# Transposed scores and reordered norms in the first batch of a cross-covariance attention and feed-forward kernel

## The chip, the cores and the metric

The kernel runs on one core of one Trainium2 chip. A core has TensorE for matmuls (PE in the profile, with its weight loads as PEld), VectorE (DVE), ScalarE (ACT), GpSimd (POOL, which here mostly issues DMAs) and SyncE (SP, likewise). They run independently and wait for one another on semaphores. Sixteen DMA engines move data between HBM and the on-chip memory SBUF; matmuls write into PSUM.

The metric is device time in microseconds (us), lower is better. The span of a profile, from the first to the last instruction, is a little shorter than the measured time.

## The reference

Two parts in a row. Cross-covariance attention makes, for each of 4 batches, a 256 x 256 matrix from q and k, and multiplies v with it. A feed-forward part with squared relu follows.

```python
B, N, C = (4, 6080, 256)
qn = q / (np.linalg.norm(q, axis=1, keepdims=True) + 1e-06)
kn = k / (np.linalg.norm(k, axis=1, keepdims=True) + 1e-06)
s = kn.transpose(0, 2, 1) @ qn / tau          # 256 x 256 per batch
s = s - s.max(-1, keepdims=True)
a = np.exp(s)
a /= a.sum(-1, keepdims=True) + 1e-09
x = (v @ a)                                   # then (24320, 256)

h = x @ w_in                                  # (256, 2048)
r = np.maximum(h, 0.0)
g = moe_s * (r * r) + moe_b
out = g @ w_out                               # (2048, 256)
```

The norms are taken over the 6080 rows, so each of the 256 columns of q and of k has one norm for a batch. They, and the scores, need all rows of q and k: nothing of a batch's feed-forward part can start before its last rows are there.

## The kernel before

The kernel folds the attention matrix into the first weights: it computes `wa = softmax(...) @ w_in`, so that `h = v @ wa` (line 641 of its source), squares the relu, and computes `g @ w_out` (lines 687, 713, 809; for most groups of 512 rows in a form with seven instead of eight half-size products). The attention of batch 0 comes first, as a prologue. That of batches 1 to 3 is spread, a step at a time, over the feed-forward work of the batch before.

q and k come in chunks of 512 rows (128 partitions x 4 rows x 256), cast to fp16 by the DMA; the first two chunks come as fp32 and are cast on DVE and ACT. In batch 0 the last rows make two chunks of 2 rows a partition. The scores are collected in one PSUM tile, with k as the stationary operand:

```python
def mm(self, c, j):
    ...
    for ch in range(CH):
        po(nc.tensor.matmul(
            self.s_ps[:, ch, :],
            kc[:np_, j, ts(ch, P)],
            qc[:np_, j, :],
            ...
```

`po` keeps an instruction in the order of the program. For the norms, k is squared on ACT and q on DVE; DVE folds the four rows of a partition into one, and PE sums over the partitions with a column of ones (one column of output a matmul):

```python
def squares(a, js):
    def f():
        ...
        if a == 0:
            po(nc.vector.tensor_mul(sq[:np_, 0, js, :], qc[:np_, js, :], qc[:np_, js, :]))
        else:
            po(nc.scalar.activation(out=sq[:np_, 1, js, :], in_=kc[:np_, js, :], func=AF.Square))
...
def add_norms(self, arrays=(0, 1), last=False):
    ...
        for i, (t, np_, j, ch) in enumerate(todo):
            po(nc.tensor.matmul(self.n_ps[a][:, ch : ch + 1], t[:np_, a, j, ts(ch, P)],
                                ones16[:np_, 0:1], ...))
```

In batch 0 every chunk's folded rows are summed on PE; in later batches an accumulating DMA adds them to the first chunk's rows (`into_first`).

The norms are roots by `Ln` and `Exp(0.5 x)` on ACT; DVE adds EPS and takes the reciprocal. The scores are scaled by k's inverse norms and must be turned over so that q's columns lie on the partitions: on PE in batch 0 (`turn`), in later batches by splitting into two fp16 parts and transposing those with DMAs (`split`, `join`). `exps` then applies q's inverse norms as the activation's scale:

```python
def scale():                                   # batch 0
    for ch in range(CH):
        po(nc.vector.tensor_scalar_mul(out=st["s"][:, ch], in0=self.s_ps[:, ch],
                                       scalar1=st["r"][:, 1, ch : ch + 1]))
def turn():
    ...
    for ch in range(CH):
        for j in range(CH):
            po(nc.tensor.transpose(st["t"][j][:, ts(ch, P)], st["s"][:, ch, ts(j, P)], ident32))
def exps(j):
    po(nc.scalar.activation(out=st["e"][:, j, :], in_=st["t"][j], func=AF.Exp,
                            scale=st["r"][:, 0, j : j + 1]))
def sums():                                    # row sums r_ps, reciprocal rs
    ...
def fold_mm(f0, n, m, wa_ps):                  # wa = e.T @ w_in, then scaled by rs
    ...
```

The prologue's program order, with matmuls on idle data (`keep_busy`, called fillers below) between the chunks:

```python
NFILL = 3
FILL = {-9: 2, -8: 2, -7: 2, -6: 4, -5: 4, -4: 4, -3: 2}
...
for c in range(NCH0 - 2):
    ops = g0.norm_ops(c)
    if c >= NCH0 - 3:
        g0.add_norms()
    for j in range(g0.chunks[c][2]):
        g0.mm(c, j)
    fill = FILL.get(c - NCH0, 0)
    if fill:
        keep_busy(fill, ...)
    for f in ops:
        f()
...                                            # k's squares and norms of the last two chunks
fin[0]()
fin[1]()
keep_busy(NFILL, ...)
for c in (NCH0 - 2, NCH0 - 1):
    ops[c - NCH0 + 2][1]()                     # q's squares
    for j in range(g0.chunks[c][2]):
        g0.mm(c, j)
for f in fin[2:5]:                             # q's norms, scale, reciprocal
    f()
fin[5]()                                       # turn
transpose_v(0)
keep_busy(2, w_in16[:, 0, :P], w_in16[:, 0, :NW])
for f in fin[6:12]:                            # exps, sums, first parts of wa
    f()
```

Of the kernel before, what the change touches and what calls it, by code (L numbers as in the profile page):

```python
# [16 lines left out]
def kernel(  # L17
# [32 lines left out]
    SHIFT = 3  # L50
    assert CH == 2 and FT == 16
# [14 lines left out]
    sq_pool = pool("sq_pool", 2)  # L66
    f3_pool = pool("f3_pool", 13)
# [41 lines left out]
    class Gram:  # L109
# [32 lines left out]
        def mm(self, c, j):  # L142
            qc, kc = self.tiles[c]
            _, np_, jc = self.chunks[c]
            for ch in range(CH):
                po(nc.tensor.matmul(  # L146
                    self.s_ps[:, ch, :],
                    kc[:np_, j, ts(ch, P)],
                    qc[:np_, j, :],
                    start=(c == 0 and j == 0 and ch == 0),  # L150
                    stop=(c == len(self.chunks) - 1 and j == jc - 1 and ch == CH - 1),
                    skip_group_check=True,
                ))

        def norm_ops(self, c):
# [4 lines left out]

            def squares(a, js):
                def f():
                    if "sq" not in st:
                        st["sq"] = sq_pool.tile([P, 2, JC, C], FP16, tag="sq", name="sq")
                    if a == 0:
                        po(nc.vector.tensor_mul(  # L166
                            st["sq"][:np_, 0, js, :], qc[:np_, js, :], qc[:np_, js, :]))
                    else:
                        po(nc.scalar.activation(  # L169
                            out=st["sq"][:np_, 1, js, :], in_=kc[:np_, js, :], func=AF.Square))  # L170
                return f

            def fold(half, arrays, last):
                def f():
# [10 lines left out]
                    if last and (self.b == 0 or c == 0 or c == len(self.chunks) - 1):  # L185
# [4 lines left out]
            def into_first():  # L190

                dst, src = self.rows[0][0][0][:np_], st["f", 1][:np_]
                po(nc.gpsimd.dma_start(out=dst, in_=src, accum_op=ALU.add))  # L193

            def unfolded():
                for rows in self.rows:
                    rows.append((st["sq"], np_, jc))
# [5 lines left out]
            if jc == 2:  # L203
# [4 lines left out]
            return ops + [into_first] if self.b > 0 and 0 < c < len(self.chunks) - 1 else ops  # L208

        def add_norms(self, arrays=(0, 1), last=False):  # L210

            if self.b > 0:

                self.n_all = x_tile[0][:, 1, : 2 * CH].rearrange("p (a c) -> p a c", a=2)
                self.n_ps = [self.n_all[:, 0], self.n_all[:, 1]]
            for a in arrays:
                first = self.n_ps[a] is None
                if first:
                    self.n_ps[a] = ps_o.tile([P, 2, C], FP32, tag="o_ps", name="n_ps")[:, 0, :CH]
                todo = [(t, np_, j, ch) for t, np_, jc in self.rows[a] for j in range(jc)  # L220
                        for ch in range(CH)]
                self.rows[a].clear()
                for i, (t, np_, j, ch) in enumerate(todo):
                    po(nc.tensor.matmul(self.n_ps[a][:, ch : ch + 1], t[:np_, a, j, ts(ch, P)],
                                        ones16[:np_, 0:1], start=(first and i == 0),
                                        stop=(last and i == len(todo) - 1),
                                        skip_group_check=True))

        def finish_ops(self):
# [3 lines left out]
            def root(out, sums):  # L233

                po(nc.scalar.activation(out=out, in_=sums, func=AF.Ln, bias=tiny))
                po(nc.scalar.activation(out=out, in_=out, func=AF.Exp, scale=0.5))

            def norms(a=None):

                if "r" not in st:  # L240
                    st["nrm"] = sm_pool.tile([P, 2, CH], FP32, tag="nrm", name="nrm")
                    st["r"] = sm_pool.tile([P, 2, CH], FP32, tag="rnrm", name="rnrm")
                if a is None:
                    self.add_norms(last=True)
                    root(st["nrm"], self.n_all)
                else:
                    self.add_norms((a,), last=True)
                    root(st["nrm"][:, a], self.n_ps[a])

            def recip(a=None):  # L250
                own = slice(0, 2) if a is None else slice(a, a + 1)
                nrm, r = st["nrm"][:, own], st["r"][:, own]
                po(nc.vector.tensor_scalar_add(out=nrm, in0=nrm, scalar1=EPS))
                po(nc.vector.reciprocal(out=r, in_=nrm))
                if inv_tau != 1.0 and a != 1:
                    po(nc.vector.tensor_scalar_mul(
                        out=st["r"][:, 0], in0=st["r"][:, 0], scalar1=inv_tau))

            def scale():
                st["s"] = sm_pool.tile([P, CH, C], FP32, tag="sm_s", name="sm_s")  # L260
                for ch in range(CH):
                    po(nc.vector.tensor_scalar_mul(
                        out=st["s"][:, ch], in0=self.s_ps[:, ch],
                        scalar1=st["r"][:, 1, ch : ch + 1]))


            def split(part):
                st[part] = sm_pool.tile([P, CH, C], FP16, tag=f"s_{part}", name=f"s_{part}")
                rk = st["r"][:, 1]
                if part == "hi":  # L270
                    po(nc.vector.tensor_mul(
                        st["hi"], self.s_ps, rk[:, :, None].broadcast_to((P, CH, C))))
                else:
                    for ch in range(CH):
                        po(nc.vector.scalar_tensor_tensor(
                            out=st["lo"][:, ch], in0=self.s_ps[:, ch], scalar=rk[:, ch : ch + 1],
                            op0=ALU.mult, in1=st["hi"][:, ch], op1=ALU.subtract))
                st[part + "T"] = sm_pool.tile([P, CH, C], FP16, tag=f"t_{part}", name=f"t_{part}")
                for ch in range(CH):
                    po(nc.sync.dma_start_transpose(  # L280
                        out=st[part + "T"][:, :, ts(ch, P)], in_=st[part][:, ch, :]))

            def join():
                t_sb = sm_pool.tile([P, CH, C], FP32, tag="sm_s", name="t_sb")
                po(nc.vector.tensor_add(t_sb, st["hiT"], st["loT"]))
                st["t"] = [t_sb[:, j, :] for j in range(CH)]

            def turn():

                st["t"] = [h_tile("t_ps")[:, 0, :C], self.bank("t_ps", CH, C)[:, 0, :]]  # L290
                for ch in range(CH):
                    for j in range(CH):
                        po(nc.tensor.transpose(
                            st["t"][j][:, ts(ch, P)], st["s"][:, ch, ts(j, P)], ident32))

            def exps(j):
                if j == 0:
                    st["e"] = sm_pool.tile([P, CH, C], FP16, tag="eT", name="eT")
                po(nc.scalar.activation(
                    out=st["e"][:, j, :], in_=st["t"][j], func=AF.Exp,  # L300
                    scale=st["r"][:, 0, j : j + 1]))
# [53 lines left out]
            if self.b == 0:  # L355
                front = [lambda: norms(1), lambda: recip(1), lambda: norms(0),
                         scale, lambda: recip(0), turn]
            else:
                front = [norms, recip]
                front += [lambda: split("hi"), lambda: split("lo"), join]  # L360
# [46 lines left out]
    ident32 = consts.tile([P, P], FP32)  # L407
    make_identity(nc, ident32)
# [12 lines left out]
    nc.vector.memset(tiny, 1e-30)  # L421
    for c in range(NDIRECT):
        g0.load(c)
        g0.cast(c)
    for c in range(NDIRECT, len(g0.chunks) - 2):
        g0.load(c)

    for parts in ((0,), (1,)):
        for c in range(len(g0.chunks) - 2, len(g0.chunks)):
# [7 lines left out]
    load_w_in(0, NW)  # L437
    load_v(0)
    load_w_in(NW, 2 * NW)
# [20 lines left out]
    NFILL = 3  # L460
    FILL = {-9: 2, -8: 2, -7: 2, -6: 4, -5: 4, -4: 4, -3: 2}

    def keep_busy(n, w, x):

        idle_ps = h_tile("idle_ps")[:, 0, :]
        for _ in range(n):
            po(nc.tensor.matmul(idle_ps, w, x, start=True, stop=True, skip_group_check=True))

    fin = g0.finish_ops()
    for c in range(NCH0 - 2):  # L470
        ops = g0.norm_ops(c)
        if c >= NCH0 - 3:
            g0.add_norms()
        for j in range(g0.chunks[c][2]):
            g0.mm(c, j)
        fill = FILL.get(c - NCH0, 0)
        if fill:
            keep_busy(fill, g0.tiles[c][1][:, 0, :P],
                      g0.tiles[c][0][:, :2, :].rearrange("p j c -> p (j c)"))
# [3 lines left out]
    ops = [g0.norm_ops(c) for c in (NCH0 - 2, NCH0 - 1)]  # L483
    g0.add_norms()
    for k_squares, _, into_rows in ops:
        k_squares()
        into_rows()
    fin[0]()
# [412 lines left out]
```

## Time and profile before

| what | value |
|---|---|
| time, median of 3 runs | 719.0 us (719.0 to 719.15) |
| span of the profile | 717.2 us, 17629 instructions |
| first h matmul (line 641) | 38.60 us |
| scores, PE line 146 | 384 matmuls, 69.6 us |
| ACT squares, line 169 | 49, 50.4 us, 1033 ns each |
| DMA, whole span | 84.25 MB, mean 117 GB/s |
| DMA, first 38.6 us | 221 GB/s |

How to read it: a group's line gives the source line, the engine, what is written from what, the count, the busy time and the mean of one. A timeline's line gives the start, the duration, engine and line, the operation, and in brackets how long the engine was idle before and what ended that. The chain of waits runs back from the last instruction through whatever released each step, and is printed in order of time: start, duration, engine, line. The "granted clock" is what the throttle allowed TensorE, as a share of full speed.

### The profile page before, as it was taken

The numbers are of one execution on the slowest core, as the hardware profiler recorded it, in microseconds if no ns is written. First come the engines' busy times: TensorE is split into PE (matmuls) and PEld (weight loads), VectorE is DVE, ScalarE is ACT, GpSimd is POOL, SyncE is SP. The second block draws the span as 40 slices with busy tenths as digits, with TensorE's granted clock in tenths as the row PEclk, the third lists the DMA queues.
The fourth block names the chain that finished last, engine by engine and source line by source line (L and its number), as shares of the span: only waits on it lengthen the run. The fifth ranks groups of instructions, "written<-read, shape, count | busy, mean of one in ns | idle before, by whom it ended". The sixth has DMA issues, their size and how long they took to land.

```text
span 717.2 us, 17629 instructions
## 1 busy us (share of the span) xinstructions
PE 698.9 (97%) x7479; PEld 504.6 (70%) x7479; DVE 626.1 (87%) x882; ACT 536.5 (75%) x579; POOL 109.8 (15%) x189
## 2 busy tenths in 40 slices
PE   4799999999999999999999999999999999999998
PEld 2556777776677777777677777777668777777777
DVE  4879999999789999999889899999887888888886
ACT  4479877787777777777777778777877777777875
POOL 4532332101201222111110222110000000000000
PEclk9999999999999999999999999999999999999999
DMA  9999998647556879443972877944423333321201
GB/s 236 207 259 172 159 170 137 111 108 129 119 107 114 144 133 145 108 93 83 154 151 57 141 138 124 154 90 86 105 63 75 93 71 74 97 60 46 83 30 74
DMA packets 89790, 84.25 MB, mean 117 GB/s; under 512 B 59664, under 2 KB 64848, under 8 KB 89712
## 3 DMA queue, kind: packets, MB, share of 16 engines
q0 software_dynamic: 26064, 43.40, 37.5%
q1 hardware_dynamic: 63072, 38.43, 21.5%
q8 instruction: 58, 0.95, 0.6%
q10 hardware_dynamic: 576, 1.31, 0.5%
q14 instruction: 20, 0.16, 0.1%
HBM read 78.91 MB, written 24.90 MB: 145 GB/s over the span
## 4 chain that ended last, share of the span: by engine, by line
PE 93%; DMA 4%; DVE 1%; ACT 1%; POOL 1%; issue 0%; POOLq 0%; ACTq 0%
PE h_ps L641 45%; PE o_ps L809 40%; PE s_ps L146 4%; DMA qk<-in_q_dram 3%; PE wa_ps L326 2%; DMA v<-in_v_dram 1%; PE o_ps L713 1%; PE o_ps L687 0%; POOL qk L130 0%; ACT r L651 0%; DVE o_sb L669 0%; DVE S L737 0%; DVE sq L166 0%; DVE S L735 0%; DVE S L739 0%
## 5 line engine op out<-in xcount | busy, mean ns | idle before, releaser
L651 ACT ACTIVATE r<-h_ps 128x1024 f16<-128x1024 f32 (+1 forms) x384 | 388.4, 1014 | 153.4 <-PE h_ps L641 150.9
L641 PE MATMUL h_ps<-vT,wa 128*128 128x512 f16 (+7 forms) x1632 | 452.1, 364 | 0.1
L809 PEld LDWEIGHTS <-S 128*128 128x128 f16 x2944 | 198.0, 98 | 85.0 <-issue 0.9
L809 PEld LDWEIGHTS <-g 128*128 128x128 f16 x2208 | 155.0, 98 | 74.1
L664 DVE TENSOR_TENSOR g<-r 128x2048 f16<-128x2048 f16 (+2 forms) x150 | 174.8, 1165 | 14.6 <-ACT r L651 14.5
L809 PE MATMUL o_ps<-T,S 128*128 128x128 f16 x2208 | 183.3, 219 | 0.1
L641 PEld LDWEIGHTS <-wa 128*128 128x128 f16 x1632 | 135.9, 98 | 20.6 <-ACT wa L319 0.3
L809 PE MATMUL o_ps<-w_out,g 128*128 128x128 f16 x1472 | 134.2, 219 | 0.2 <-DVE u L669 0.2
L669 DVE SCALAR_TENSOR_TENSOR o_sb<-o_ps,s_out,u 128x256 f32<-128x256 f32 x138 | 66.5, 482 | 47.1 <-PE o_ps L809 44.5
L662 ACT ACTIVATE g<-r 128x1024 f16<-128x1024 f16 (+1 forms) x97 | 100.4, 1035 | 0.2
L146 PE MATMUL s_ps<-qk 128*128 128x256 f16 (+1 forms) x384 | 69.6, 281 | 14.0 <-ACT qk L137 8.7
L379 POOL DMA_DIRECT2D v<-in_v_dram x48 | 31.3, 656 | 263.5 <-DMA vT<-v 209.6
L669 DVE SCALAR_TENSOR_TENSOR u<-o_ps,s_out,rowconst 128x256 f32<-128x256 f32 x138 | 66.0, 478 | 0.0
L809 PE MATMUL o_ps<-w_out,S 128*128 128x128 f16 x736 | 63.5, 219 | 0.0
L809 PE MATMUL o_ps<-N,g 128*128 128x128 f16 x736 | 63.4, 219 | 0.0
L193 POOL DMA_DIRECT2D f<-f x30 | 26.3, 877 | 225.6 <-DVE f L182 172.0
L169 ACT ACTIVATE sq<-qk 128x1024 f16<-128x1024 f16 (+3 forms) x49 | 50.4, 1033 | 10.0 <-DMA qk<-in_k_dram 6.7
L737 DVE TENSOR_TENSOR S<-S,g 128x2048 f16<-128x2048 f16 (+1 forms) x47 | 56.4, 1201 | 1.3
L735 DVE TENSOR_TENSOR S<-g 128x2048 f16<-128x2048 f16 (+1 forms) x47 | 56.1, 1193 | 0.0
L741 DVE TENSOR_TENSOR S<-g,S 128x2048 f16<-128x2048 f16 x46 | 56.0, 1217 | 0.0
L739 DVE TENSOR_TENSOR S<-g 128x2048 f16<-128x2048 f16 x46 | 55.9, 1216 | 0.0
L146 PEld LDWEIGHTS <-qk 128*128 128x128 f16 (+1 forms) x384 | 32.8, 101 | 20.1 <-DVE qk L136 8.0
(74 smaller groups left out, 314.9 us busy)
## 6 DMA issues: line engine op xcount, KB each, us to landing
out_dram<-o_sb SPq DMA_DIRECT2D x46, 512.0 KB, 3.0
v<-in_v_dram POOLq DMA_DIRECT2D x47, 256.0 KB, 4.7
qk<-in_k_dram POOLq DMA_DIRECT2D x42, 256.0 KB, 6.1
qk<-in_q_dram POOLq DMA_DIRECT2D x42, 256.0 KB, 7.2
f<-f POOLq DMA_DIRECT2D x30, 128.0 KB, 3.1
vT<-v SPq DMA_TRANSPOSE x182, 3.2
w<-in_moe_w_out_dram POOLq DMA_DIRECT2D x4, 512.0 KB, 11.3
raw<-in_k_dram SPq DMA_DIRECT2D x2, 512.0 KB, 6.4
```

What stands on the lines that cost most here:

```text
L146: po(nc.tensor.matmul(self.s_ps[:, ch, :], kc[:np_, j, ts(ch, P)], qc[:np_, j, :], start=(c == 0 and j == 0 and ch == 0), stop=(c == len(s ...
L169: po(nc.scalar.activation(out=st["sq"][:np_, 1, js, :], in_=kc[:np_, js, :], func=AF.Square))
L641: po(nc.tensor.matmul(dst, wa[:, ci, ts(m, P)], src, start=(ci == 0), stop=(ci == CH - 1), skip_group_check=True))
L651: po(nc.scalar.activation(out=r16[:, :, i % 2, :n], in_=h_tiles.pop((g, i))[:, :, :n], func=AF.Relu))
L662: po(nc.scalar.activation(out=dst, in_=src, func=AF.Square))
L664: po(nc.vector.tensor_mul(dst, src, src))
L669: po(nc.vector.scalar_tensor_tensor(out=dst, in0=src, scalar=s_out, op0=ALU.mult, in1=add, op1=ALU.add))
L735: po(nc.vector.tensor_add(T[1], A21, A22))
L737: po(nc.vector.tensor_sub(T[2], T[1], A11))
L739: po(nc.vector.tensor_sub(T[3], A11, A21))
L741: po(nc.vector.tensor_sub(T[4], A12, T[2]))
L809: po(nc.tensor.matmul(st[name][:, j, :], a()[:, i, ts(j, P)], w[:, i, :], start=first, stop=last, skip_group_check=True))
```

## The change

The change touches the attention part, for the most part batch 0.

- The operands of the score matmul are exchanged, so that the scores come out with q's columns on the partitions, as the exponential wants them. The transposes on PE, and the split, the transposing DMAs and the join of the later batches, are left out.
- k's norms then lie along the free dimension. They are wanted in every partition, so k's sums are taken with a 128 x 128 matrix of ones as the stationary operand and 256 columns of output; q's sums stay as they were.
- The inverse norms come from ACT alone: Ln, Exp(0.5 x), Ln with EPS as bias, Exp(-x). Add and reciprocal on DVE are left out.
- In batch 0 both q and k are squared on ACT, apart from the last three chunks, whose q squares and small k squares are DVE's. DVE folds them and adds the folded rows to those of the first chunk, so that PE sums one tile and not one for each chunk.
- The last three chunks (`NLATE`) have k's rows loaded ahead of q's, and k's norms are finished before q's last rows come. The first v tile is loaded ahead of w_in, whose first 512 columns come in two pieces.
- The fillers are left out, apart from two of 256 columns before the first parts of wa. One identity matrix (fp32) is no longer made.
- In later batches the finishing steps are laid out anew (`FIN`, `fin_len` 56 instead of 54).

The diff, cut to its core; cuts are marked with "...":

```diff
@@ mm
-                    kc[:np_, j, ts(ch, P)],
-                    qc[:np_, j, :],
+                    qc[:np_, j, ts(ch, P)],
+                    kc[:np_, j, :],
@@ norm_ops
+            at_end = self.b == 0 and c >= len(self.chunks) - NLATE
...
-                    if a == 0:
+                    if a == 1 and at_end and jc < JC:
+                        po(nc.vector.tensor_mul(
+                            st["sq"][:np_, 1, js, :], kc[:np_, js, :], kc[:np_, js, :]))
+                    elif a == 0 and (self.b > 0 or at_end):
                         po(nc.vector.tensor_mul(
                             st["sq"][:np_, 0, js, :], qc[:np_, js, :], qc[:np_, js, :]))
                     else:
                         po(nc.scalar.activation(
-                            out=st["sq"][:np_, 1, js, :], in_=kc[:np_, js, :], func=AF.Square))
+                            out=st["sq"][:np_, a, js, :], in_=(qc, kc)[a][:np_, js, :],
+                            func=AF.Square))
...
             def into_first():
-                dst, src = self.rows[0][0][0][:np_], st["f", 1][:np_]
-                po(nc.gpsimd.dma_start(out=dst, in_=src, accum_op=ALU.add))
+                dst, src = self.first[:np_], st["f", 1][:np_]
+                if self.b == 0:
+                    po(nc.vector.tensor_add(dst, dst, src))
+                else:
+                    po(nc.gpsimd.dma_start(out=dst, in_=src, accum_op=ALU.add))
@@ add_norms
+                if a == 1:
+                    po(nc.tensor.matmul(self.n_ps[1], ones16[:np_, :], t[:np_, 1, j],
+                                        start=start, stop=end, skip_group_check=True))
+                    continue
...
@@ finish_ops: root, recip, split, join, turn go
+            def inverse(a):
+                def part(i):
+                    ...
+                    func, kw = [(AF.Ln, dict(bias=tiny)), (AF.Exp, dict(scale=0.5)),
+                                (AF.Ln, dict(bias=eps)), (AF.Exp, dict(scale=-1.0))][i]
+                    po(nc.scalar.activation(out=r, in_=r if i else self.n_ps[a], func=func, **kw))
...
+            def scale(halves=1):
+                ...
+                    po(nc.vector.tensor_mul(st["t"][:, js], self.s_ps[:, js],
+                                            rk[:, None, :].broadcast_to((P, n, C))))
...
@@ loads
-    load_w_in(0, NW)
     load_v(0)
+    load_w_in(0, 2 * P)
+    load_w_in(2 * P, NW)
@@ prologue
-    NFILL = 3
-    FILL = {-9: 2, -8: 2, -7: 2, -6: 4, -5: 4, -4: 4, -3: 2}
...
+    for c in range(NCH0 - NLATE):
         ops = g0.norm_ops(c)
-        if c >= NCH0 - 3:
-            g0.add_norms()
         for j in range(g0.chunks[c][2]):
             g0.mm(c, j)
...
+    for c in late:
+        k_squares, _, into_rows = ops[c]
         k_squares()
-        into_rows()
+        into_rows(1)
+        g0.add_norms(1)
+    for f in last_sums:                        # last fold and add of chunk NCH0 - 4
+        f()
...
+    for f in (norms_k, *inverse_k):
+        f()
+    for c in late:
+        ops[c][1]()                            # q's squares
+        ops[c][2](0)
         for j in range(g0.chunks[c][2]):
             g0.mm(c, j)
+        if c == NCH0 - 1:
+            norms_q()
+        else:
+            g0.add_norms(0)
+    for f in inverse_q:
         f()
+    scale_s()
     transpose_v(0)
-    keep_busy(2, w_in16[:, 0, :P], w_in16[:, 0, :NW])
+    keep_busy(w_in16[:, 0, :P], w_in16[:, 0, : 2 * P])
+    keep_busy(w_in16[:, 0, :P], w_in16[:, 0, : 2 * P])
...
-    FIN = (0, 3, 5, 7, 15, 17, 19, 22)
+    FIN = (0, 0, 3, 5, 7, 16, 16, 17, 18, 19, 20, 24, 26, 29)
```

## The prediction

> **What bounds the kernel now.** First the page: busy time by engine and the slices, to see which engine fills the span and where it does not.
>
> ```profile
> PE 698.9 (97%) x7479; PEld 504.6 (70%) x7479; DVE 626.1 (87%) x882; ACT 536.5 (75%) x579; POOL 109.8 (15%) x189
> ...
> PE   4799999999999999999999999999999999999998
> ```
>
> TensorE (PE) is full from the fourth slice on. A busy PE need not be a PE at its peak, so I asked for the busy time by stretch, cut where the first matmul of the feed-forward part starts (38.60 us in the timeline).
>
> ```profile
> 0.00:38.60 38.60, 23.88 (x206) 16.10 (x206) 24.32 (x50) 18.24 (x24) 20.16 (x41) 1.00 1.06 221
> 38.60:60.00 21.40, 21.35 (x130) 12.29 (x131) 17.91 (x31) 18.92 (x22) 4.47 (x9) 1.00 1.09 226
> 60.00:700.00 640.00, 639.67 (x6961) 463.48 (x6959) 572.30 (x782) 491.19 (x522) 85.18 (x140) 1.00 0.57 109
> 700.00:717.20 17.20, 13.96 (x189) 12.71 (x186) 11.55 (x22) 8.20 (x14) 0.00 (x0) 1.00 0.21 77
> ```
>
> The columns are length, then PE, weight loads, DVE, ACT and POOL with counts, then granted clock, DMA share and GB/s. From 60 to 700 us PE is idle for 0.33 us of 640. The stretches around the later batches' changeovers (150 to 200, 330 to 380, 510 to 560 us) have 50.00 of 50 us. So what the change does for batches 1 to 3, on DVE, ACT or in transposes, has no idle PE to recover. Only the first 38.6 us can move: a prologue, then a full PE stream whose length the change hardly touches.
>
> The chain of waits says what the prologue is:
>
> ```profile
> 4.35 11.56 DMA qk<-in_q_dram
> ...
> 18.76 9.74 DMA qk<-in_q_dram
> 28.50 0.28 issue
> 28.78 7.72 DMA v<-in_v_dram
> 36.50 0.05 issue
> 36.55 0.62 PE vT_ps L390 x8
> 37.17 0.43 PE idle_ps L467 x2
> 37.60 0.08 PE r_ps L309 x4
> 37.68 0.90 PE wa_ps L326 x8
> 38.57 0.02 issue
> 38.60 0.60 PE h_ps L641 x2
> ```
>
> Loads of q and k up to 28.5 us, then v, then a few matmuls. The timeline has a second path beside it, almost as long, from the last rows of q to the exponentials:
>
> ```profile
> 34.00 0.24 DVE L253 TENSOR_SCALAR nrm<-nrm 128x2 f32<-128x2 f32 x1 [1.08 <-ACT nrm L236]
> ...
> 34.35 0.74 DVE L166 TENSOR_TENSOR sq<-qk 128x512 f16<-128x512 f16 x2
> ...
> 35.44 0.26 ACT L235 ACTIVATE nrm<-n_ps,tiny 128x2 f32<-128x2 f32 x1 [1.47 <-PE n_ps L224]
> ...
> 36.43 0.84 ACT L299 ACTIVATE eT<-t_ps,rnrm 128x256 f16<-128x256 f32 x2 [0.50 <-PE t_ps L293]
> ```
>
> DVE runs in order and sits 1.08 us behind ACT's root of k's norms before it may square q's last rows. The exponentials end at 37.27, and v's transposes and the two fillers at 37.60: removing either path alone gains at most 0.3 us.
>
> [...] records of the 128x256 score matmul are 418 ns at 7 to 13 us and 272 ns from 14.3 us, after a run that began at 10.61. No trace here shows PE falling back, since the fillers kept it busy. The granted-clock column reads 1.00 throughout, so this is read from durations. [...] the trace's 128x2048 f16 products take 1218. So folds, squares and the new in-place add cost what the same shapes cost now. [...] The trace's 128x2 Ln takes 0.26 us, and the 128x256 exponential 0.47 from PSUM and 0.50 from SBUF. [...] the trace has one table load, at the start.
>
> **The change part by part.**
>
> *Loads.* Same bytes. In the steady part a 512 KB piece lands every 1.25 us (q's pieces release PE at 26.0 and 28.5, with one of k between). I put k's last large piece at 29.8 (its square starts at 29.82) and q's last piece at 34.0, estimated back from v at 36.5 in two steps of 1.25. Reordered, I estimate k's pieces at 29.8, 30.55 and 31.15, and q's at 32.4, 33.2 and 34.0. v now precedes w_in, so it lands about 35.25 instead of 36.5, and the first quarter of w_in near 36. Its transposes (0.62 us) then end before the exponentials, which takes v off the chain.
>
> *Squares on ACT.* Ten chunks at two 128x1024 squares: three back to back took 2.94 us, so 0.98 each, 1.96 a chunk against 2.5 us between chunks. ACT starts late (10.5 us, after its second cast) with four chunks waiting: twenty squares from 10.5 at 0.98 is 30.1, just behind the last of these q pieces at 28.5. It catches up only at the end. DVE: folds of 0.69 and 0.42 plus a new add of 0.42 is 1.53 a chunk instead of 0.68+0.69+0.42 = 1.79. Both fit under the loads.
>
> *k's norms early.* Last fold 30.0 to 30.7, two k squares (0.40 each) to 31.55, fold and add (0.42 each) to 32.45, nine ones matmuls of 256 columns finishing near 32.8. Then four dependent 128x256 activations; from 0.47 for one of this shape I estimate 1.85 us: k's inverse norms by 34.7.
>
> *q's end.* PE must do eight score matmuls, ten one-column sums, four score matmuls, four sums, again four and four. From 32.8, with 0.107 us a score matmul (eight in 1.03 us with the drain) and 28 ns a sum (forty in 1.14), the last sum is near 35.1 and ready at 35.25. The sum on PE binds rather than the landing at 34.0. Then four 128x2 activations in place of Ln, Exp, add and reciprocal: 0.26+0.20+0.26+0.20 plus gaps, about 1.0, against 0.94 now (35.44 to 36.34 with handovers). Exponentials start 36.0 to 36.3 instead of 36.43, since the inverse norms now bind. DVE scales in two halves of 0.48 from 34.95, so this is done at 35.9. It replaces the two scalings and four fp32 transposes (0.74 us), the path that ended at 36.38.
>
> *To the first h matmul.* Exponentials from SBUF take 0.50 each instead of 0.42 apart, ending 37.0 to 37.3; the present stretch from r_ps at 37.44 to h_ps at 38.60, 1.16 us, stays. First h matmul: 38.2 to 38.5. Gain 0.1 to 0.4 us; I take 0.35 with the earlier first load issue (one identity fewer on POOL).
>
> *After that.* For each later batch, eight one-column sums (0.22 us) become two of 256 columns and four of one (0.33): 0.3 us more PE in all. Gone are DVE's 0.68+0.95+0.69+0.34 us, about 2.7, and four transposing DMAs, against a product of about 0.7 and some 1.4 us more ACT; DVE and ACT have room there. The wait for w_in's last half (40.5 us) is met, since its fold comes at about 41. Sum: 719.0 - 0.35 + 0.3 = 718.95. A shorter DVE queue may take back part of the 0.33 us that PE idles from 60 to 700; I give it half, 0.15: **718.8 us**.
>
> **Rivals.** *PE goes cold.* Without fillers PE works 0.86 us in each 2.5. Every gap is near 1.6 us[...]; but the least that PE was seen to stay warm on is 0.86+0.43 of 2.5. If cold, the sixteen last score matmuls take 0.21 us, the q sums end about 1.5 us later, and the stream starts 1 to 2 us late: 720 to 720.6. [...] *ACT becomes the bound.* If ACT's backlog does not close by 30 us, k's sums and four long activations slip one for one: 719 to 720. For it: only 0.5 us a chunk to spare; against: the count above. *The loads hide it all.* If v and w_in land no sooner, nothing moves: 719.0 to 719.3. *DVE relief pays.* If PE in the steady part has waits that the busy column hides, 717.5 is possible; 0.33 us idle of 640 speaks against.
>
> **Range and chances.** Most of the weight lies on a shift of under half a microsecond either way; perhaps three in ten on a cold or late prologue worth 1 to 2 us. So 717.6 to 720.4. Two per cent is 14.4 us, over a third of the prologue, and nothing found reaches it.
>
> **What would show it.** In the profile after: score matmul records of 272 ns from 16 to 35 us (warm) or 418 (cold); v's transposes before 36.2; ACT's ones-summed Ln near 32.9; exponentials starting 36.0 to 36.3; the first h matmul at 38.2 to 38.5; PE idle under 1 us from 60 to 700. The prediction is wrong if the first h matmul lies after 39, or if the stream from there to the end is not within 0.5 us of the present 678.6 (717.2 - 38.6) with the 0.3 added.

## The result and the profile after

The changed kernel takes 724.2 us (median of 5 runs, 723.88 to 725.31) against 719.03 us: a ratio of 1.0074, 95% interval 1.0062 to 1.0087. It is 0.7% slower, within 2%, and outside the predicted range of 717.6 to 720.4.

The page of the kernel after: busy time by engine, and from the 40 slices those of PE and of the clock that the throttle granted, in tenths.

```profile
PE 700.7 (97%) x7413; PEld 504.4 (70%) x7413; DVE 619.6 (86%) x863; ACT 550.5 (76%) x609; POOL 110.3 (15%) x188
...
PE   4799999999999999999999999999999999999997
PEclk9699999999999999999999999999999999999999
```

PE is 97% busy, as before. Its clock has a dip in the second slice (18 to 36 us). Busy time by stretch of the kernel after, cut at its first h matmul (39.35 us):

```profile
0.00:39.35 39.35, 22.92 (x146) 14.99 (x146) 20.77 (x46) 27.59 (x36) 20.53 (x40) 0.83 1.08 221
39.35:60.00 20.65, 20.59 (x126) 11.72 (x126) 17.23 (x30) 18.22 (x21) 4.47 (x9) 1.00 1.08 223
60.00:700.00 640.00, 637.52 (x6896) 460.74 (x6894) 565.58 (x762) 492.62 (x538) 85.33 (x140) 1.00 0.59 108
```

The prologue is 0.75 us longer (39.35 against 38.60 us). From there to the end the stream takes 723.5 - 39.35 = 684.15 us, where it took 717.2 - 38.60 = 678.6: **5.55 us more**. The busy column shows 2.48 us of PE idle from 60 to 700 us, against 0.33, so it explains less than half of that.

**Where the stream lost it.** I set the start of each relu activation (384 in each kernel, in the same order) against its counterpart before. The delay is 0.75 us at the first, and nearly the same up to 88 us. For batch 1 it grows by 0.53 us between 88 and 142 us and by 1.28 at the finishing steps. For batches 2 and 3 it grows by 0.18 before and by 1.38 at the finishing steps, each time. That is 4.93 us, in a few places, three times over. The other 0.64 us comes after the last matmul: from its start to the end of the span it is 4.11 us, and 3.47 before.

**What happens there.** The timeline of the kernel after at batch 1's finishing steps (start, duration, engine and line, operation; weight loads and work of no bearing are cut):

```profile
146.13 0.55 PE L789 MATMUL o_ps<-T,S 128*128 128x128 f16 x7
146.23 0.48 DVE L649 SCALAR_TENSOR_TENSOR u<-o_ps,s_out,rowconst 128x256 f32<-128x256 f32 x1
...
146.76 0.38 PE L236 MATMUL o_ps<-f,ones 128*128 128x256 f16 x2
...
146.98 0.59 PE L621 MATMUL h_ps<-vT,wa 128*128 128x512 f16 x2
...
147.41 0.39 PE L789 MATMUL o_ps<-T,S 128*128 128x128 f16 x4
147.58 0.47 ACT L256 ACTIVATE r<-o_ps,tiny 128x256 f32<-128x256 f32 x1
...
148.11 0.33 PE L789 MATMUL o_ps<-T,S 128*128 128x128 f16 x3 [0.31 <-ACT r L256]
```

In later batches the sums for the norms (L236, the matmul with ones) have no PSUM tile of their own. They use the free second half of the tile, called X here, that collects four of a group's seven products. The trace shows two waits there. The sums come after DVE has emptied X's last product (the `u` row, which ends at 146.71; they begin at 146.76), and PE's next product in X comes after ACT's Ln (L256) has read the sums (it ends at 148.05; the product begins at 148.11). The halves do not overlap, and PE waits all the same. No kernel here let the two go on at once, so what the waits guard against is not shown.

Now the arithmetic. From the starts of successive matmuls in an undisturbed stretch of the stream of this kernel, one of 128 columns takes 0.056 us, one of 256 columns 0.109, one of 512 columns 0.216. A gap below is what a start comes later than this allows. The seven from 146.13 are through at 146.52, and the sums begin at 146.76: 0.24 us lost. The four from 147.41 are through at 147.63, and the next begins at 148.11: 0.48 us lost. For q, batch 2 has 0.23 and 0.38 in the same way. **Together 1.33 us a batch, about 4.0 us in three.**

The columns hide most of it. The record of a matmul lasts some 0.16 us beyond its place in the stream (seven take 0.39, the row says 0.55). So the bracket shows 0.31 of the 0.48, and the 0.24 shows as nothing. PE's waits in the kernel after, summed from 60 us to the end (total us, times, longest), name Ln six times, and once something else:

```profile
PE o_ps L789 <- ACT r L256: 1.6, 6, 0.3
PE o_ps L789 <- DVE o_sb L649: 0.2, 1, 0.2
```

**A third place.** That last wait is at 139 us, where the delay grows before the finishing steps. The timeline there, DVE's rows and PE's:

```profile
138.59 0.69 DVE L191 TENSOR_TENSOR f<-sq 112x1024 f16<-112x1024 f16 x1
...
139.18 0.33 PE L789 MATMUL o_ps<-T,S 128*128 128x128 f16 x3
139.19 0.48 DVE L649 SCALAR_TENSOR_TENSOR o_sb<-o_ps,s_out,u 128x256 f32<-128x256 f32 x1
...
139.72 0.38 PE L789 MATMUL o_ps<-w_out,S 128*128 128x128 f16 x4 [0.21 <-DVE o_sb L649]
```

DVE takes a fold of the norms' rows first and only then empties the tile whose other half PE wants next (`o_sb`). By starts this costs 0.38 us. The same order, fold and then emptying, stands with a gap of 0.16 at 89, 241, 285, 415 and 459 us. In the kernel before the emptying at this place comes at 137.54, with no fold ahead of it, and PE goes on without a gap.

The kernel before at the place of the sums:

```profile
146.49 0.55 PE L809 MATMUL o_ps<-T,S 128*128 128x128 f16 x7
...
146.88 0.34 PE L224 MATMUL o_ps<-ones,f 128*128 128x1 f16 x8
...
147.09 0.59 PE L641 MATMUL h_ps<-vT,wa 128*128 128x512 f16 x2
147.27 0.26 ACT L235 ACTIVATE nrm<-o_ps,tiny 128x4 f32<-128x4 f32 x1
...
147.58 0.50 PE L809 MATMUL o_ps<-T,S 128*128 128x128 f16 x6
```

Here the sums stand in the middle of a product that is itself collected in X: DVE had emptied X long before (its `u` row ran from 144.97 to 145.45), and 146.49 + 7 x 0.056 = 146.88 leaves no gap. Ln has 4 columns and takes 0.26 us; it ends at 147.53, under the h matmuls (147.09 + 2 x 0.216 = 147.52), so PE loses 0.06. What the change did is two things: `fin_len` 56 with the new `FIN` moved the sums to just after DVE's turn on X, and 256 columns for k made the Ln 0.47 us. In the kernel after the Ln also comes late, at 147.58, behind a square on ACT (1.06 us from 146.64).

**The prologue.** The chain of waits of the kernel after, from k's last squares to the first h matmul:

```profile
30.98 2.08 PE n_ps L236 x9
33.06 1.71 PE s_ps L148 x8
34.76 0.24 PE n_ps L240 x10
35.01 0.57 PE s_ps L148 x4
...
35.66 0.46 PE s_ps L148 x4
...
36.23 0.27 ACT r L256
...
36.77 0.30 ACT r L256
...
37.33 0.92 ACT eT L277 x2
...
38.52 0.90 PE wa_ps L304 x8
39.41 0.54 PE h_ps L621 x2
```

v is off the chain, as meant. Eight score matmuls take 1.71 us, where they should take 0.87 (8 x 0.109): from start to start 0.213 us each from 32.85 us on, where it was 0.109 within the bursts at 16 and 18 us. The clock is why; stretches of two microseconds of the kernel after, PE's row alone (length, busy with count, granted clock, DMA share, GB/s):

```profile
20.00:22.00 2.00, 0.92 (x7) 0.87 1.12 208
22.00:24.00 2.00, 0.96 (x5) 0.50 1.14 212
...
32.00:34.00 2.00, 2.00 (x11) 0.50 1.19 206
34.00:36.00 2.00, 2.00 (x28) 0.72 1.35 202
```

Without fillers PE fell to half rate (granted clock 0.50) at about 21.5 us and was back at 35.1, too late for the path that counts. Not every execution is like this one. Over the whole span the mean granted clock was 0.991 in the runs of 725.24 (the profiled one) and 725.31 us, and 0.995 in the other three, of 723.88 to 724.2. The two kinds lie about a microsecond apart, and the median is of the second: its span of 722.4 us less the stream would put its first h matmul at 38.3 (an estimate), no later than before. So the loss of the median lies in the stream.

### The profile page after: what moved, and what is told of

Read it like the earlier page. It is cut to its first block, busy times and chain, and to the rows that moved or that the text cites. A ratio compares the mean times of both kernels' runs of the same rounds, so it can differ in the third digit from the quotient of the medians.

```text
span 723.5 us, 17474 instructions
## 1 busy us (share of the span) xinstructions
PE 700.7 (97%) x7413; PEld 504.4 (70%) x7413; DVE 619.6 (86%) x863; ACT 550.5 (76%) x609; POOL 110.3 (15%) x188
## 4 chain that ended last, share of the span: by engine, by line
PE 89%; ACT 4%; DMA 3%; DVE 3%; issue 1%; SPq 0%; ACTq 0%
PE h_ps L621 43%; PE o_ps L789 38%; PE s_ps L148 4%; PE wa_ps L304 2%; ACT sq L177 1%; DMA qk<-in_k_dram 1%; DMA raw<-in_q_dram 1%; ACT r L631 1%; DVE S L717 1%; PE o_ps L693 1%; DVE S L715 1%; ACT g L642 1%; PE o_ps L667 0%; DMA vT<-v 0%; DVE o_sb L649 0%
## 5 line engine op out<-in xcount | busy, mean ns | idle before, releaser
L148 PE MATMUL s_ps<-qk 128*128 128x256 f16 (+1 forms) x384 | 73.9, 296 | 14.8 <-ACT qk L139 9.1
L177 ACT ACTIVATE sq<-qk 128x1024 f16<-128x1024 f16 (+1 forms) x57 | 57.9, 1048 | 0.0
```

Source lines behind the costliest of these rows:

```text
L148: po(nc.tensor.matmul(self.s_ps[:, ch, :], qc[:np_, j, ts(ch, P)], kc[:np_, j, :], start=(c == 0 and j == 0 and ch == 0), stop=(c == len(s ...
L177: po(nc.scalar.activation(out=st["sq"][:np_, a, js, :], in_=(qc, kc)[a][:np_, js, :], func=AF.Square))
```

## The experiments

Two questions: what costs the stream 5.55 us (theory: where the sums stand in the seven products and what waits on X, called the bank theory in the expectations, with X as the bank; rivals: the added work on PE, ACT and DVE in itself, or something carried over from the prologue), and what the prologue is worth warm (theory: the clock, called the cold theory; rival: the loads hide it anyway). "First h" is the start of the first h matmul; "stream" is the span of the profile less first h; both come from the profile of the run.

| kernel | first h | stream | median us | ratio to before (95%) |
|---|---|---|---|---|
| before | 38.60 | 678.6 | 719.03 | |
| after | 39.35 | 684.15 | 724.2 | 1.0074 (1.0062 to 1.0087) |
| e1_fin54 | 39.49 | 680.51 | 721.34 | 1.0029 (1.0018 to 1.0040) |
| e2_norm10 | 38.19 | 683.11 | 723.53 | 1.0066 (1.0049 to 1.0083) |
| e3_fill | 38.88 | 684.12 | 724.63 | 1.0076 (1.0061 to 1.0091) |
| e4_before_fin56 | 38.77 | 680.83 | 721.56 | 1.0038 (1.0023 to 1.0053) |
| e6_ln_sbuf | 39.18 | 681.52 | 722.44 | 1.0039 (1.0024 to 1.0054) |
| e7_before_nofill | 41.15 | 678.45 | 720.99 | 1.0022 (1.0012 to 1.0032) |
| h1_first_only | 39.20 | 678.4 | 719.09 | 0.9995 (0.9987 to 1.0003) |
| h2_first_only_fill | 38.12 | 678.48 | 719.01 | 0.9993 (0.9985 to 1.0001) |
| e8_fin_plus2 | 38.05 | 681.35 | 721.92 | 1.0037 (1.0023 to 1.0051) |
| e9_fin54_fill | 38.32 | 680.48 | 720.86 | 1.0026 (1.0015 to 1.0037) |
| f1_two_steps | 38.27 | 678.43 | 718.43 | 0.9987 (0.9980 to 0.9993) |

### One number undone: `fin_len` back to 54

```diff
-        fin_len = 56
+        fin_len = 54
```

> The changed kernel with the finishing steps of batches 1 to 3 begun two steps later (fin_len 54 as before, not 56), so that both sets of norm sums fall inside the third product, where the bank of X has already been emptied, instead of between two products. Bank theory (PE stands still at the norm sums: about 0.24 us for the emptying of X and 0.23 to 0.31 us for ACT's Ln, twice for each later batch): the first wait goes, and the second shrinks for q; 0.6 to 0.8 us less for each batch, so 721.8 to 722.4. Rival (the longer activations of 128x256 delay ACT, wherever they stand): 724.0 to 724.4.

721.34 us, slightly better than expected; the stream is 3.64 us shorter. Two of the number shift all finishing steps by two steps of the feed-forward work, and with them the sums. They also change the stretch over which the chunks of q and k are spread, and so when their folds come. PE's gaps at the sums fall from 1.33 to 0.40 us a batch (0.29 for k, 0.11 for q), and the fold no longer stands ahead of the emptying at 139 us and at the like places of batches 2 and 3.

### The same number changed in the kernel before

```diff
-        fin_len = 54
+        fin_len = 56
```

> The kernel before with only fin_len 56 instead of 54, so that its norm sums stand between two products as in the changed kernel. Bank theory: one stall of about 0.3 to 0.5 us for each of three batches, total 720.0 to 720.6. Rival (the position does not matter, the changed kernel's added work does): 719.0 to 719.2.

721.56 us, beyond the 720.0 to 720.6 expected: with nothing else changed, **one number costs the kernel before 2.5 us**. Gaps of 0.23 and 0.29 us now stand around its sums, 0.52 a batch against 0.06, which is (0.52 - 0.06) x 3 = 1.4 us of the stream's 2.23. The other 0.8 is not at the sums but at the places of the third kind: here too DVE takes a fold first (138.01) and empties the tile after it (138.61), and PE stands still for 0.38 us.

### Another place for the sums, with fin_len 56 kept

```diff
-    FIN = (0, 0, 3, 5, 7, 16, 16, 17, 18, 19, 20, 24, 26, 29)
+    FIN = (4, 4, 6, 8, 10, 20, 20, 21, 22, 23, 24, 26, 28, 31)
```

> The changed kernel with the norm sums of batches 1 to 3 four steps later (first entries of FIN 4 instead of 0, 20 instead of 16), where X has been emptied a step before and is next written a step and a half after. Bank theory: both waits go for both arrays, the stream from the first h matmul is back at 678.6 to 679.3 us from 684.2, total 719.2 to 720.2. Rival (ACT's longer activations, or more PE work): 723.5 to 724.4.

A miss: 723.53 us, where 719.2 to 720.2 was expected. Four steps later the sums stand after another of X's products, and DVE is late in emptying that too. Of the waits of PE in this kernel from 60 to 700 us, those at k's sums (L236) and q's (L240):

```profile
PE o_ps L236 <- DVE u L649: 1.0, 3, 0.3
PE o_ps L240 <- DVE u L649: 1.0, 3, 0.3
```

This time the wait for DVE is long enough to be seen, as 0.33 us each, at all six places; by starts it is 0.50. The wait for Ln is gone. I had taken any place away from the old one to be good. The miss says that the place has to be inside one of X's products.

### Two steps later, which is the place they had before

```diff
-    FIN = (0, 0, 3, 5, 7, 16, 16, 17, 18, 19, 20, 24, 26, 29)
+    FIN = (2, 2, 5, 7, 9, 18, 18, 19, 20, 21, 22, 26, 28, 31)
```

> The changed kernel with every entry of FIN two steps later and fin_len left at 56, so that the norm sums of batches 1 to 3 fall inside the third product as with fin_len 54, and the score matmuls keep the spacing of the changed kernel. If the place of the sums is what costs: stalls of some 0.4 us a batch in place of 1.33, stream about 681.3 to 681.8, total 720.8 to 721.9. If the spacing that fin_len sets is what costs: stream 683.5 or more, total over 723.

As expected: the stream is 681.35 us, 2.8 shorter, with `fin_len` at 56. The timeline of PE in this kernel at batch 2's sums of k, and ACT's row:

```profile
319.69 0.55 PE L789 MATMUL o_ps<-T,S 128*128 128x128 f16 x7
320.08 0.38 PE L236 MATMUL o_ps<-f,ones 128*128 128x256 f16 x2
320.30 0.60 PE L621 MATMUL h_ps<-vT,wa 128*128 128x512 f16 x2
321.02 0.49 PE L789 MATMUL o_ps<-T,S 128*128 128x128 f16 x6
```
```profile
320.50 0.47 ACT L256 ACTIVATE r<-o_ps,tiny 128x256 f32<-128x256 f32 x1
```

The sums begin at 320.08 = 319.69 + 7 x 0.056: no wait for DVE. What is left is 0.29 us for the Ln, which ends at 320.97, while the h matmuls are through at 320.73. With q's 0.11 it is 0.40 us a batch against 1.33: (1.33 - 0.40) x 3 = 2.8 us, just what the stream gained. **The place of the sums is the cause of half of the loss**, and the gaps at the sums account for all of this half. The gap of 0.38 us at the third place is still there (138.0 us).

### Ln freed from X

```diff
-                    po(nc.scalar.activation(out=r, in_=r if i else self.n_ps[a], func=func, **kw))
+                    src = r if i else self.n_ps[a] if self.b == 0 else ones32[:, : CH] if a == 0 else wide
+                    po(nc.scalar.activation(out=r, in_=src, func=func, **kw))
```

(`wide` is a 128x256 tile of ones in SBUF. This leaves out the real norms of batches 1 to 3: the sums are made on PE, but not used.)

> The changed kernel in which the first Ln of the inverse norms of batches 1 to 3 reads a constant in SBUF and not the sums in PSUM, so that it leaves out the norms of those batches; sums and all activations are done all the same. Bank theory: PE no longer waits for ACT before it writes X again, 0.38 to 0.48 us twice for each batch, so 2.2 to 2.8 us less, 721.4 to 722.0; the wait for the emptying of X (0.24 us twice a batch) stays. Rival (ACT's added work delays the relu): 724.0 to 724.4.

The stream is 2.63 us shorter, as expected; 722.44 us is 0.4 above the expected range. What is left at the sums is the wait for DVE, 0.23 + 0.24 us a batch: (1.33 - 0.47) x 3 = 2.6. So with the sums where the change puts them, the Ln's hold on X is worth 2.6 us, and the wait for DVE 0.47 x 3 = 1.4.

### Only batch 0 changed

```diff
-    grams = {b: Gram(b, ...) for b in range(B)}
+    grams = {b: Gram(b, chunks_first) if b == 0 else GramOld(b, chunks_later) for b in range(B)}
```

(`GramOld` is the class of the kernel before, with its `FIN` and `fin_len`.)

> The change in batch 0 alone: batches 1 to 3 keep the scores, norms, steps and transposing DMAs of the kernel before (fin_len 54 and its FIN). Bank theory: the stream from the first h matmul is 678.5 to 678.9 us again, so only the prologue differs: first h matmul at 38.2 to 39.5 us according to when PE falls back to half rate, total 718.6 to 720.0. Rival (the prologue's new order also costs later, through the loads or a longer DVE queue): stream 680 or more, total over 721.

As expected: a stream of 678.4 us, as before, and 719.09 us in all, not to be told from the kernel before. All of the 5.55 us comes with the later batches' part of the change, none of it from something carried over from the prologue. Busy time from 60 to 700 us in this kernel:

```profile
60.00:700.00 640.00, 639.68 (x6956) 463.33 (x6955) 572.69 (x782) 491.57 (x523) 85.38 (x140) 1.00 0.59 109
```

PE is idle 0.32 us there again.

### Fillers put back

In the loop over batch 0's chunks of the kernel after:

```diff
             g0.mm(c, j)
+        for _ in range(FILL.get(c - NCH0, 0)):      # {-9: 2, -8: 2, -7: 2, -6: 4, -5: 4, -4: 4}
+            keep_busy(g0.tiles[c][1][:, 0, :P], g0.tiles[c][0][:, :2, :]...)
```

> The changed kernel with the fillers of before put back behind the score matmuls of six chunks of batch 0, nothing else. Cold theory (PE fell to half rate at 21.5 us and did q's last sums 1 us late): score matmul records of 272 ns up to the end, first h matmul at 38.2 to 38.5 instead of 39.35, total 723.0 to 723.4. Rival (k's inverse norms on ACT set the end of the prologue): first h matmul stays at 39.2 to 39.4, total 724.0 to 724.3. What happens to later batches stays as it is, 684 us of stream.

Half a miss. The clock held at 1.00 and score matmuls stayed at 272 ns, but the first h came at 38.88 and the median did not gain. In the profiled execution q's second-to-last rows were late; the timeline's row for their square:

```profile
34.45 0.76 DVE L174 TENSOR_TENSOR sq<-qk 128x512 f16<-128x512 f16 x2 [1.52 <-DMA qk<-in_q_dram]
```

DVE stood idle for 1.52 us for a load issued at 25.12 that took 9.31 us. So in this execution the loads held the prologue back.

> The same with the fillers of before behind six chunks of batch 0. Cold theory: PE stays at full rate, first h matmul at 38.2 to 38.4, total 718.5 to 718.8, faster than before by some 0.3 us and steadier than without fillers. Rival (the loads of q's last rows come later with fillers, as one profile had it): first h matmul near 38.9, total 719.2 to 719.6.

The same fillers with only batch 0 changed: exponentials at 36.10 us and first h at 38.12, within what I expected, and a span of 716.6 us. The median, 719.01, is no better than before and 0.2 above what I expected. The profiled execution was the fastest of the 13 (718.41), so its 0.48 us is not typical. The rival of this expectation, later loads with fillers, has some support: q's last piece landed 7.0 us after its issue in all six traces of the changed prologue without fillers, and 7.0, 8.0, 8.3 and 8.3 us in the four with them. So few traces do not show that fillers delay the loads.

> The whole change with both repairs: fin_len 54, and the fillers of before behind six chunks of batch 0. Bank theory and cold theory together: stream 679.9 as with fin_len 54 alone, first h matmul at 38.2 to 38.9, total 719.9 to 720.6, still slower than before, since Ln over 256 columns keeps PE from X for 0.3 us a batch. If the two do not add: 721.3 as with fin_len 54 alone.

Fillers and `fin_len` 54 together: 720.86 us, slightly above the expected range. It is 0.5 us below `fin_len` 54 alone, within the spread of the runs. The stream is that of e1 (680.48), not the 679.9 that I had written down. Fillers alone had gained nothing in the median, so that the two gains add is not shown.

### Fillers taken out of the kernel before

```diff
-        if fill:
+        if False:
...
-    keep_busy(NFILL, ...)
```

> The kernel before without its fillers, but for the two of 512 columns on w_in. Cold theory: PE falls back to half rate at about 21 us here too, matmul records of 418 ns until 33 to 35 us, first h matmul 0.3 to 1.2 us later, total 719.3 to 720.2. Rival (fillers cost as much as they save): 718.6 to 719.1.

First h at 41.15 us in the profile, 2.5 later and twice what I allowed, and a median of 720.99 (718.91 to 722.19). The granted clock fell twice in the profiled execution: to 0.50 from 24.0 to 30.9 us, and again from 34.3 to 41.1, so that the first parts of wa ran at half rate too. The stream is unchanged. So the fillers were worth about 2 us to the kernel before. To the changed batch 0 they are worth 1.1 us at the first h of the profile (39.20 in h1, 38.12 in h2) and nothing in the medians (719.09 and 719.01): in h1 the clock was back at 34.4 us, in time for the first h. Both profiles are also off their medians, h1's above (719.44) and h2's below.

### Two steps instead of four for q's inverse norms

On the kernel of h2, for q in batch 0: Ln, then Exp with a scale of -0.5. This leaves out the EPS of 1e-6 that the reference adds to q's norms.

> The change in batch 0 alone with fillers, and q's inverse norms of batch 0 by two activations in place of four (Ln, then Exp(-0.5 x)); it leaves out the EPS of 1e-6 there. Theory (the inverse norms of q end the prologue): exponentials 0.5 us sooner, first h matmul at 37.6 to 37.9, total 718.3 to 718.6. Rival (the scaling by DVE or the loads set it): at most 0.1 us, total 718.9 to 719.1.

718.43 us, as expected, a ratio of 0.9987 (0.9980 to 0.9993): **below the kernel before**, whose median beside it was 719.11, and 0.6 us below h2. ACT's timeline of this kernel:

```profile
35.71 0.26 ACT L260 ACTIVATE r<-n_ps,tiny 128x2 f32<-128x2 f32 x1 [1.18 <-PE n_ps L240]
36.01 0.20 ACT L260 ACTIVATE r<-r 128x2 f32<-128x2 f32 x1
36.24 0.91 ACT L281 ACTIVATE eT<-sm_t,r 128x256 f16<-128x256 f32 x2
```

The exponentials follow the first Ln by 0.53 us. In the kernel after, with four steps, it is 1.10 (36.23 to 37.33). The first h, 38.27, missed the expected 37.6 to 37.9: q's second-to-last piece landed at 34.38 in this execution, where it came at 32.78 in h2's. The fair partner is e3, with the same prologue but for the two steps and with that piece as late (34.43). Against it the exponentials (36.24, there 36.85) and the first h (38.27, there 38.88) come 0.61 us sooner, about as much as the medians of f1 and h2 differ.

## Why the prediction was wrong

**The step that failed**: "So what the change does for batches 1 to 3, on DVE, ACT or in transposes, has no idle PE to recover", and after it the term "0.3 us more PE in all" for the stream. From a PE without idle time I took that nothing could be gained, and then priced only the matmuls added. A stream without gaps can lose, and here a wait newly put in it was paid in full: from the kernel after to e8 the gaps at the sums and the stream shrink by the same 2.8 us. Nor was it without gaps: by starts, the kernel before stands still for some 1.9 us from 60 to 700, where the busy column showed 0.33. I had listed the new `FIN` and `fin_len` in the change but gave them no line in the sum. I did not ask in which PSUM tile the sums of the later batches lie, though the code says it, nor who reads it when. The mis-sized term, 0.3, measured 5.55. Its parts:

| part of the 5.55 us | us | from |
|---|---|---|
| sums placed after DVE's turn on X, Ln behind a square | 2.8 | after to e8, gaps and stream alike |
| Ln where the sums stand well (k's with 256 columns, q's own): 0.40 against 0.06 us of gaps a batch | 1.0 | rows of e8 and e1 against before |
| more columns in the sums: 2 x 0.109 + 4 x 0.028 against 8 x 0.028 | 0.3 | counted, as predicted |
| `fin_len` 56 apart from the sums' place: a fold ahead of the emptying of a tile that PE wants | 0.8 | e8 to e1, gaps and stream alike; e4 has the same 0.8 |
| end of the program, from the start of PE's last matmul | 0.6 | 4.11 us against 3.47 |

The last row is what e1 also has: 680.51 - 678.6 = 1.91, less 1.0 and 0.3. All seven kernels with the change in the later batches have 4.10 to 4.13 us there, and all six without it 3.45 to 3.47. The trace shows what SyncE does in it. At the end it waits, in the same order in both kernels, for the semaphores of the DMAs. In the kernel before the last store has the semaphore that stands last in this order, and that wait ends 2.56 us after the start of the last matmul (716.25 and 713.68 us). In the kernel after its semaphore stands fifth from the end: that wait ends 2.60 us after (721.96 and 719.36), four more follow it, and the last ends 3.20 us after. That the place of the last store's semaphore shifts because the transposing DMAs are gone is my guess, and not shown.

Both signs of being wrong that the prediction named came true: the first h matmul lies after 39, and the stream is off by more than 0.5. **"PE idle under 1 us from 60 to 700"** failed too (2.48), and the busy column showed under half of what was lost. The busy share of PE, 97% in both kernels, showed none of it.

**The clock.** I gave the cold prologue three chances in ten, on the ground that each gap was near 1.6 us. That PE stays warm through gaps so short was my estimate, and the runs went against it: the clock fell to 0.50 in all seven profiles of kernels without fillers, and in none of the six with them. Its price in the profile of the kernel after is 39.35 - 38.12 (h2, warm) = 1.2 us at the first h matmul, within the 1 to 2 us that the rival named. Against e3, warm but with late loads, it is 0.5. q's sums were ready at 36.23 and not 35.25, exponentials at 37.33 and not 36.0 to 36.3, first h at 39.35 and not 38.2 to 38.5.

**Right, where warm.** With PE warm early enough, the steps came out as worked: exponentials at 36.10 (h2) and 36.17 (e2, whose clock happened to return earlier, at 32.7 us); first h at 38.05 to 38.32 in e2, e8, e9, h2. ACT's twenty squares, counted from 10.5 to 30.1 us, ran from 10.79 to 29.83. k's Ln came at 33.09 for 32.9. v left the chain; it landed at 34.60 for an expected 35.25, and the first piece of w_in at 35.35 for 36. The gain of 0.35 us was about right in these profiles (0.3 to 0.55); no median shows it. That PE's sums and not the landing of q bind was right in e2 and e8, where q's last piece landed at 33.27. With fillers it landed at 34.2 in h2 and at 34.6 to 34.7 in e3 and f1, and there PE and DVE waited for it. In the kernel before, DVE's wait for k's root was not what held q's last rows, as the prediction reads it: they landed at 34.33 and were squared from 34.35.

**The other rivals.** ACT as the bound did not happen in the prologue, and ACT did matter where it was not looked for: a late Ln holds PE (0.48 us at 147.63). "DVE relief pays" was wrong in sign: DVE has 6.5 us less to do, and PE waits on it more, because of when, not how much.

## What to carry to other kernels

In a stream that leaves the bounding engine no idle time, price the position of each inserted step, not only its work: for every PSUM tile it touches, ask who emptied the tile last and who has to read it before the next writer (here 0.24 and 0.48 us at one place). A schedule constant that shifts everything by two steps is a change of its own (2.5 us in e4); try it alone first. Where matmul records overlap, take the gaps from the starts of successive rows and the time of one matmul, since the idle and wait columns showed less than half of them here (2.15 us more of idle and 1.8 of waits, where the gaps grew by 2.8 + 1.0 + 0.8 = 4.6). And ask what stands in an engine's queue ahead of the row that frees a tile: a fold of 0.69 us there cost PE up to 0.38.

## What the runs showed of the hardware

PE's clock fell without a long pause. In the kernel after, from 16.07 us on, PE worked in bursts of 1.05 us every 2.5 us or so, about 41% of the time, and was never idle for more than 1.52 us by its records; from about 21.5 us the granted clock was 0.50. In e8, with the same bursts from 16.0 us, it fell at 25.5. With two fillers more a chunk (in h2 1.48 us of 2.5, about 58%) it held at 1.00.

The length of the cold stretch varied as well. Worked out from the mean clock of stretches of 1 or 2 us, the clock stood at 0.50 for 13.6 to 13.7 us in the kernel after, e1 and e6, for 6.8 us in e2, e8, e7 (twice) and h1, and for 3.4 us in a second fall of h1. With dense work from about 32 us in each, it was back at 35.1 us in the kernel after, at 35.3 in e1 and at 32.7 in e2. The end of the prologue went with it: in the five kernels with the same batch 0 and no fillers, the first h matmul came at 38.05 us (e8, back at 32.4), 38.19 (e2, 32.7), 39.18 (e6, 34.9), 39.35 (after, 35.1) and 39.49 (e1, 35.3).
